# Attention, a dense feed-forward layer and routed experts in one kernel: weights joined in PSUM, the first tiles reordered, w_out split later, P of four tiles turned by TensorE

## The chip, the cores and the metric

One core of one Trainium2 chip runs the whole program. The metric is the device time of one execution in microseconds; the time before is 1401.77 us, the median of three runs (1400.38 to 1402.29).

## The reference, cut to what matters

```
# attention: B=8, H=8, S=576, D=64; k and v are averaged over runs of 8 rows (72 remain)
scores = matmul(q, mean8(k).T) / 8 ; attn = softmax(scores) ; x = attn @ mean8(v)     # x: 4608 x 512
# dense layer: w_in 512 x 2048, w_out 2048 x 512
h = x @ w_in ; g = where(h >= 1, h, where(h <= -1, 0, (h+1)**2 / 4)) ; x = g @ w_out
# routed layer: 8 experts, 512 -> 1024 -> 512, each token goes to the expert of its largest logit
out = gate * (relu(x @ w1[e]) @ w2[e])
```

The weights w_in and w_out arrive as 64-bit floats. The kernel reads them as two 32-bit words and makes a 32-bit float of each pair itself.

## The kernel before, in words

The 4608 tokens are 36 tiles of 128, in ten blocks (`BLK`): three tiles, seven blocks of four, three, two. A product in 32-bit accuracy is three matmuls: every operand is kept as a high and a low part, and high by high, high by low and low by high are added up.

**Blocks.** For block j and each of the 16 slices m of the hidden width, `f1(j, m)` is the first product (12 matmuls, L593 to L595) with its activation: L600 on VectorE, L601 on ScalarE, L605 on VectorE, L606 on ScalarE (high part) and `low_part`, L264, on VectorE. `f2(j, m)` is the second product (L621 to L623). The loop over `steps` calls `f1` two steps ahead of `f2`; between them `slot` puts in the attention of the next block's tiles (`units`), conversions of weights, and routing. Called functions append work to `later` and `pend`; `flush` and `mix` issue it. That writing order is the order in each engine's queue.

**A tile's attention** (`tile_units`): `u_qt` transposes q, `u_sc_all` makes the scores (L312), takes maxima and differences on VectorE (L319, L321) and the exponential on ScalarE (L326); `finish` sums (L376), adds 1e-9 (L378), takes the reciprocal (L379) and multiplies (L382 or L390 on GpSimd); P is transposed; `u_pv` multiplies by V (L425) and writes the block's input XT, high part on ScalarE (L431), low part on VectorE (L432). Two ways exist to transpose P. `u_pt` uses TensorE (L412) and ScalarE (L414). `u_turn_p` and `u_place_p` use two VectorE block transposes (L396, L398), a store to DRAM (p_d) and three loads back. `turned(t)` chooses: through DRAM for tiles 3 to 6 and 9 to 33.

**Weights** are converted in block 0 and ahead of it, 32 pieces in the table `order`: w_in 0 to 3, w_out 0 and 1, and so on. For piece n, `tick` issues `convert_a(n)` on ScalarE (L527: the high words, scaled, into the destination; L531: their signs), `convert_b(n)` on VectorE (L539: low word shifted and joined with the sign, both read from SBUF, written to the PSUM bank `CV`; L542: the destination shifted and joined with CV) and, for piece n-2, `convert_c` (L549 on ScalarE: high part; L264 on GpSimd: low part). For w_out both parts are also stored to DRAM (`wo_d`, 512 KB a piece), and from block 1 on `load_out` loads them for each slice.

**First tiles.** Tiles 0 to 2 come before any product of the dense layer. Keys and values are pooled by `head_pool` (L249 on VectorE, L252 to L254 on GpSimd) or by TensorE (`u_kp`), and five pieces of weights have been through `convert_a` when the first product starts.

Of the kernel before, what the change touches and what calls it, by code (L numbers as in the profile page):

```python
# [24 lines left out]
def attention_ffn_routed_experts_kernel(  # L25
# [12 lines left out]
    nc = tc.nc  # L38
# [70 lines left out]

    KB = [at(576 * i, 4 * SP_).rearrange("p (a c) -> p a c", a=4) for i in range(2)]  # L110
    QB = [at(1152 + 512 * i, 512) for i in range(2)]
    QB2 = at(6336, 512)
    QT = at(2176, 512)
    SC = [at(2688, 576), at(7616, 576)]
    HEAD = blocks[0][1]
    RAW = [at(3264 + 512 * i, 512, SP_) for i in range(3)]
    KP = at(4800, 512, SP_)
# [160 lines left out]
    def u_kp(b, c, raw):  # L278
# [25 lines left out]
    def u_sc_all(t):  # L304
        pbs = [bank(), bank()]
        for c in range(4):
            for g in range(2):
                toks = slice(64 * g, 64 * g + 64)
                kb = KB[(t * 128 + 64 * g) // S % 2]
                for i in range(2):  # L310
                    rows = slice(64 * i, 64 * i + 64)
                    nc.tensor.matmul(pbs[i][toks, c * SP_:(c + 1) * SP_],  # L312
                                     qt_of(t)[rows, c * 128 + 64 * g:c * 128 + 64 * g + 64],
                                     kb[rows, c], start=True, stop=True)
        sc, sc3, smx = sc_of(t), sc3_of(t), smx3[:, t % 3]
        for i in range(2):
            src = pbs[i][:, 0:4 * SP_].rearrange("p (h c) -> p h c", h=4)
            hs = slice(i, H, 2)
            nc.vector.tensor_reduce(out=smx[:, hs], in_=src, axis=AX.X, op=ALU.max)  # L319
            mix()  # L320
            nc.vector.tensor_tensor(out=sc3[:, hs], in0=src,  # L321
                                    in1=smx[:, hs].to_broadcast([128, 4, SP_]), op=ALU.subtract)
        wide[0] = True

        def exps():
            nc.scalar.activation(out=sc, in_=sc, func=ACTF.Exp, scale=1.0 / 64)  # L326
            finish(t)
# [195 lines left out]
    def convert_a(i):  # L523
        dst, rb = cvt_dst(i)
# [8 lines left out]
    def convert_b(i):  # L533
# [572 lines left out]
    with tc.manual_schedule():  # L1106

        wgp = WG.rearrange("p e d -> p (e d)")[0:SP_]
        raw0 = [WG[0:SP_, i] for i in range(8)] + RAW + [
            FX[0:SP_, 512 * i:512 * (i + 1)] for i in range(1, 5)] + [PT[:, 0]]  # L1110
# [5 lines left out]
        def run_units(n):  # L1116
            for _ in range(n):
                units.popleft()[1]()
            if qloads:
                qloads.popleft()()  # L1120

        load_q(0)
        for i in range(H):
            load_kv(0, i, raw0[i])
        load_q(1)
        load_q(2)
        for i in range(H, 2 * H):
            load_kv(0, i, raw0[i])
# [23 lines left out]
        hu[2][2]()
        head_pool(15, nc.gpsimd)
        for i in (11, 13):
            head_pool(i, nc.vector)
# [5 lines left out]
        line = [(0, 3), (0, 5), (1, 3), (0, 6), (1, 5), (2, 3), (1, 6), (2, 5), (2, 6)]
        for i, (t, n) in enumerate(line):
            hu[t][n]()
            flush()
            if i in (0, 2, 4, 6):
# [291 lines left out]
```

## Time and profile before

| | |
|---|---|
| median of three runs | 1401.77 us |
| the profiled execution's own time | 1404.79 us |
| span of its profile | 1402.8 us |
| TensorE matmul busy | 1357.5 us, 97% |
| VectorE, ScalarE, GpSimd busy | 778.1, 433.7, 358.7 us |
| first product starts | 38.11 us |
| block 1's first product starts | 146.73 us |

The page's second part cuts the span into 40 slices of 35 us. TensorE's busy tenths begin 6, 8, 7, 8 and are 9 from there to the last slice, which is 8. In a row of the timeline the columns are: start in us, duration in us, engine, line, operation, output and input, shape, count, and in brackets the idle time before and what ended it.

### The profile page before, as it was taken

How to read it: one execution, taken by the hardware profiler on the slowest of the kernel's cores; microseconds unless marked ns; L12 is line 12 of the kernel's file. 1: busy time of each engine (PE TensorE's matmuls, PEld its weight loads, DVE VectorE, ACT ScalarE, POOL GpSimd, SP SyncE). 2: the span in 40 equal slices, each digit the busy share in tenths (PEclk: the TensorE clock that was granted, in tenths of full speed). 3: DMA queues.
4: the chain of work that ended last, by engine and by line, in shares of the span. 5: the costliest groups of instructions: out<-in, count | busy, mean ns of one | idle time of the engine just before them, and what ended most of it. 6: DMA issues, size and time to landing. Idle time of an engine off the chain costs nothing. (4 is left out here: it accounts for less than half of the span.)

```text
span 1402.8 us, 22101 instructions
## 1 busy us (share of the span) xinstructions
PE 1357.5 (97%) x8082; PEld 1112.8 (79%) x8082; DVE 778.1 (55%) x1577; ACT 433.7 (31%) x729; POOL 358.7 (26%) x520
## 2 busy tenths in 40 slices
PE   6878999999999999999999999999999999999998
PEld 4767778878878778788788888888878888888786
DVE  5798556565666666575666556455532333323426
ACT  4567332222222222223222223343111111111335
POOL 5384736004304203413310011022221211111212
PEclk9999999999999999999999999999999999999999
DMA  9786647436636555545553344572543223331235
GB/s 254 226 261 240 182 136 214 129 122 194 164 124 187 153 149 168 171 155 143 165 157 111 98 152 130 192 263 72 195 129 106 91 74 113 99 111 61 79 127 187
DMA packets 170701, 213.45 MB, mean 152 GB/s; under 512 B 83432, under 2 KB 114440, under 8 KB 170569
## 3 DMA queue, kind: packets, MB, share of 16 engines
q1 hardware_dynamic: 135992, 102.29, 25.2%
q10 hardware_dynamic: 26784, 88.16, 18.8%
q0 software_dynamic: 7792, 21.35, 4.8%
q8 instruction: 69, 1.13, 0.3%
q14 instruction: 64, 0.52, 0.1%
HBM read 188.30 MB, written 47.03 MB: 168 GB/s over the span
## 5 line engine op out<-in xcount | busy, mean ns | idle before, releaser
L593 PE MATMUL ps<-XT,W 128*128 128x512 f32 (+2 forms) x640 | 243.8, 381 | 6.8 <-DVE FG L264 3.0
L595 PE MATMUL ps<-XT,W 128*128 128x512 f32 (+2 forms) x640 | 237.9, 372 | 2.7 <-POOL W L264 2.7
L594 PE MATMUL ps<-XT,W 128*128 128x512 f32 (+2 forms) x640 | 238.1, 372 | 0.2 <-DVE XT L432 0.2
L621 PE MATMUL ps<-WO,FG 128*128 128x512 f32 x576 | 231.6, 402 | 1.3 <-ACT FX L601 1.1
L622 PE MATMUL ps<-WO,FG 128*128 128x512 f32 x576 | 225.9, 392 | 0.0
L623 PE MATMUL ps<-WO,FG 128*128 128x512 f32 x576 | 225.2, 391 | 0.0
L601 ACT ACTIVATE FX<-FX,half 128x512 f32<-128x512 f32 (+2 forms) x152 | 104.0, 684 | 386.0 <-DVE FX L600 348.2
L600 DVE TENSOR_SCALAR FX<-ps 128x512 f32<-128x512 f32 (+2 forms) x152 | 96.7, 636 | 117.7 <-PE ps L595 116.9
L593 PEld LDWEIGHTS ps<-XT,W 128*128 128x128 f32 x640 | 121.8, 190 | 32.1 <-issue 3.4
L719 POOL DMA_INDIRECT perm_d<-idt,POSI x36 | 35.2, 978 | 417.6 <-DVE SM L705 353.0
L993 DVE SCALAR_TENSOR_TENSOR FG<-ps,FG 128x512 fp32r<-128x512 f32 (+1 forms) x64 | 43.2, 675 | 175.4 <-ACT FG L992 172.9
L595 PEld LDWEIGHTS ps<-XT,W 128*128 128x128 f32 x640 | 121.7, 190 | 22.3 <-POOL W L264 4.0
L605 DVE TENSOR_TENSOR ps<-FX,ps 128x512 f32<-128x512 f32 (+2 forms) x152 | 97.5, 641 | 72.8 <-ACT FX L601 71.4
L594 PEld LDWEIGHTS ps<-XT,W 128*128 128x128 f32 x640 | 121.7, 190 | 17.8 <-DVE XT L432 0.5
L621 PEld LDWEIGHTS ps<-WO,FG 128*128 128x128 f32 x576 | 108.5, 188 | 26.4 <-issue 3.0
L623 PEld LDWEIGHTS ps<-WO,FG 128*128 128x128 f32 x576 | 108.6, 188 | 23.7
L606 ACT ACTIVATE FG<-ps 128x512 fp32r<-128x512 f32 (+2 forms) x160 | 88.8, 555 | 123.9 <-DVE ps L605 112.2
L264 DVE TENSOR_TENSOR FG<-ps,FG 128x512 fp32r<-128x512 f32 (+2 forms) x160 | 100.8, 630 | 44.3 <-ACT FG L606 40.6
L622 PEld LDWEIGHTS ps<-WO,FG 128*128 128x128 f32 x576 | 108.7, 189 | 19.8
L252 POOL TENSOR_TENSOR AT<-AT 72x256 f32<-72x256 f32 x106 | 81.2, 766 | 136.3 <-DMA AT<-in_v_dram 68.7
L992 ACT ACTIVATE FG<-ps 128x512 fp32r<-128x512 f32 (+1 forms) x64 | 37.4, 584 | 244.8 <-PE ps L989 231.2
L987 PE MATMUL ps<-XT,W 128*128 128x512 f32 (+1 forms) x256 | 98.9, 386 | 2.9 <-ACT XT L971 2.5
(230 smaller groups left out, 2176.0 us busy)
## 6 DMA issues: line engine op xcount, KB each, us to landing
WO<-wo_d ACTq DMA_DIRECT2D x144, 512.0 KB
AT<-in_moe_w_dram SPq DMA_DIRECT2D x30, 1024.0 KB
p_d<-AT SPq DMA_DIRECT2D x29, 384.0 KB
AT<-in_v_dram SPq DMA_DIRECT2D x59, 144.0 KB
wo_d<-WO SPq DMA_DIRECT2D x16, 512.0 KB
AT<-in_k_dram SPq DMA_DIRECT2D x56, 144.0 KB
PT<-p_d SPq DMA_DIRECT2D x58, 128.0 KB
yrow_d<-Y ACTq DMA_DIRECT2D x7, 1032.0 KB
```

Source lines behind the costliest of these rows:

```text
L264: eng.tensor_tensor(out=lo, in0=x, in1=r32(hi), op=ALU.subtract)
L593: nc.tensor.matmul(o, wi(m, 0, c), xh, start=(c == 0), stop=False)
L594: nc.tensor.matmul(o, wi(m, 0, c), xl, start=False, stop=False)
L595: nc.tensor.matmul(o, wi(m, 1, c), xh, start=False, stop=(c == KD - 1))
L600: nc.vector.tensor_scalar(r, o, -1.0, 1.0, op0=ALU.max, op1=ALU.min)
L601: nc.scalar.activation(out=r, in_=r, func=ACTF.Square, scale=0.5, bias=half)
L605: nc.vector.tensor_tensor(out=o, in0=r, in1=o, op=ALU.max)
L606: nc.scalar.activation(out=gh, in_=o, func=ACTF.Copy)
L621: nc.tensor.matmul(o, gh, WO[:, g % 4, 0], start=(m == 0), stop=False)
L622: nc.tensor.matmul(o, gh, WO[:, g % 4, 1], start=False, stop=False)
L623: nc.tensor.matmul(o, gl, WO[:, g % 4, 0], start=False, stop=(m == KF - 1))
L987: nc.tensor.matmul(o, e1(0)[:, c, ms], xh, start=(c == 0), stop=False)
```

## The change

It has five parts.

1. **Join in PSUM.** `convert_a`'s first operation writes CV (PSUM) in place of the destination. VectorE's first join then reads CV and the sign, its second reads the low word and CV. No VectorE operation there reads two operands from SBUF. There is one CV, so piece n's first ScalarE operation has to come after piece n-1's second join; `convert_ab` sees to that order and is issued from `later`.
2. **First tiles.** q of tile 2 and the scores of tiles 0 to 2 come before the values are pooled; four heads of V are pooled by TensorE (`u_vp`) and one head of K goes from GpSimd to VectorE; two pieces of weights are through `convert_a` before the last tile's XT, and three follow after the first product. 1e-9 stands as a 73rd column of the scores, so the addition L378 is gone in all tiles.
3. **w_out.** Block 0 stores the joined 32-bit weights (`wf_d`, 256 KB a piece). In block 1 `split_out` loads a piece, splits it (ScalarE, GpSimd) and stores both parts to `wo_d`; from block 2 on they are loaded as before.
4. **P of tiles 3 to 6** goes by `u_pt`: eight TensorE transposes and two ScalarE copies a tile, in place of two VectorE transposes and four DMAs.
5. The exponential of tiles 0 to 8 is issued from `later`.

```diff
 def turned(t):
-        return TURN0 <= t < TURN1 or HEAD <= t < HEAD + blocks[1][1]
+        return TURN0 <= t < TURN1
...
+    def u_vp(more):
+
+        pb = bank()
...
+            for r in range(8):
+                nc.tensor.matmul(dst, ident[0:SP_, 0:SP_], x[:, :, r], start=(r == 0),
+                                 stop=(r == 7))
+        nc.scalar.activation(out=VS[:, 0, 0:(n + 1) * D], in_=pb[0:SP_, 0:(n + 1) * D],
+                             func=ACTF.Copy)
...
         def rest():
-            nc.vector.tensor_reduce(out=ssm, in_=sc3, axis=AX.X, op=ALU.add)
-            mix()
-            nc.vector.tensor_scalar(ssm, ssm, 1e-9, None, op0=ALU.add)
+            nc.vector.tensor_reduce(out=ssm, in_=sc4_of(t), axis=AX.X, op=ALU.add)
+            if t >= HEAD:
+                mix()
             nc.vector.reciprocal(out=ssm, in_=ssm)
...
-        nc.scalar.activation(out=dst.rearrange("p (a x) -> p a x", a=8), in_=high,
+        nc.scalar.activation(out=CV.rearrange("p (a x) -> p a x", a=8), in_=high,
                              func=ACTF.Copy, scale=2.0 ** -112)
...
-            out=ci, in0=rb[:, :, :, 0], scalar=29, in1=sg, op0=ALU.logical_shift_right,
+            out=ci, in0=ci, scalar=3, in1=sg, op0=ALU.logical_shift_left, op1=ALU.bitwise_or))
+        pend.append(lambda: nc.vector.scalar_tensor_tensor(
+            out=di, in0=rb[:, :, :, 0], scalar=29, in1=ci, op0=ALU.logical_shift_right,
             op1=ALU.bitwise_or))
-        pend.append(lambda: nc.vector.scalar_tensor_tensor(
-            out=di, in0=di, scalar=3, in1=ci, op0=ALU.logical_shift_left, op1=ALU.bitwise_or))
+
+    def convert_ab(i):
+        mix(len(pend))
+        convert_a(i)
+        convert_b(i)
...
         if o:
-            nc.sync.dma_start(out=r32(wo_d[m]), in_=r32(WO[:, m % 4]))
+            nc.sync.dma_start(out=wf_d[m], in_=dst)
...
-        for f, i in ((convert_c, n - 2), (convert_a, n), (convert_b, n)):
-            if 0 <= i < len(order) and order[i]:
-                f(i)
+        if 0 <= n - 2 < len(order) and n != 3:
+            convert_c(n - 2)
+        if n < len(order):
+            later.append(lambda: convert_ab(n))
...
+    def split_out(g):
+
+        if g < 2 * KF - 2:
+            nc.scalar.dma_start(out=WOF[(g + 2) % 4], in_=wf_d[(g + 2) % KF])
+        if g >= KF:
+            hi, lo = WO[:, g % 4, 0], WO[:, g % 4, 1]
+            nc.scalar.activation(out=hi, in_=WOF[g % 4], func=ACTF.Copy)
+            low_part(lo, WOF[g % 4], hi)
+            nc.sync.dma_start(out=r32(wo_d[g % KF]), in_=r32(WO[:, g % 4]))
...
-            if KF <= g + 1 < len(steps):
+            if KF <= g + 3 <= 2 * KF + 1:
+                split_out(g + 1)
+            elif 2 * KF < g + 2 <= len(steps):
                 load_out(g + 1)
...
         for m in range(AHEAD):
             f1(0, m)
             flush()
-            tick()
+            while ticks[0] < CAHEAD + 2 + m:
+                tick()
+                flush()
```

In the changed kernel the lines are: L546 and L550 for L527 and L531, L558 and L560 for L539 and L542, L573 for L549, L342 for L326, L433 for L414, L450 and L451 for L431 and L432, L635, L636, L640, L641 for L600, L601, L605, L606, L267 for L264.

ScalarE at the first tiles, before, from the exponential of tile 2 (L326) on; Y, AT and WG hold raw words, W is a converted weight:

```order
L326 ACTIVATE AT<-AT 128x576
L527 ACTIVATE FX<-Y 128x512
L531 ACTIVATE WG<-Y 128x512
L414 ACTIVATE FX<-ps_79 72x512
L527 ACTIVATE FX<-Y 128x512
L531 ACTIVATE WG<-Y 128x512
L414 ACTIVATE FX<-ps_72 72x512
L414 ACTIVATE PT<-ps_73 72x512
L549 ACTIVATE W<-FX 128x512
L527 ACTIVATE FX<-AT 128x512
L531 ACTIVATE WG<-AT 128x512
L431 ACTIVATE XT<-ps_74 128x4x128
```

The same place in the changed kernel:

```order
L342 ACTIVATE AT<-AT 128x8x72
L433 ACTIVATE VS<-ps_73 72x512
L433 ACTIVATE FX<-ps_74 72x512
L450 ACTIVATE XT<-ps_75 128x4x128
L546 ACTIVATE ps_78<-Y 128x512
L550 ACTIVATE WG<-Y 128x512
L433 ACTIVATE PT<-ps_76 72x512
L433 ACTIVATE PT<-ps_77 72x512
L450 ACTIVATE XT<-ps_79 128x4x128
L573 ACTIVATE W<-FX 128x512
L433 ACTIVATE FX<-ps_80 72x512
L433 ACTIVATE FX<-ps_73 72x512
```

Three pairs of conversions stood ahead of tile 0's XT copy (L431); none stands ahead of it now (L450), and one pair follows. ps_78 is CV.

ScalarE in block 0, before, from the high part of slice 7's activation (L606) to that of slice 8:

```order
L606 ACTIVATE FG<-ps_73 128x384
L326 ACTIVATE AT<-AT 128x576
L549 ACTIVATE W<-FX 128x512
L527 ACTIVATE FX<-Y 128x512
L531 ACTIVATE WG<-Y 128x512
L601 ACTIVATE FX<-FX,half 128x384
L549 ACTIVATE WO<-FX 128x512
L527 ACTIVATE FX<-AT 128x512
L531 ACTIVATE WG<-AT 128x512
L368 ACTIVATE AT<-ps_78 128x512
L606 ACTIVATE FG<-ps_72 128x384
```

The same step in the changed kernel:

```order
L641 ACTIVATE FG<-ps_74 128x384
L546 ACTIVATE ps_78<-Y 128x512
L550 ACTIVATE WG<-Y 128x512
L342 ACTIVATE AT<-AT 128x8x72
L573 ACTIVATE W<-FX 128x512
L546 ACTIVATE ps_78<-Y 128x512
L550 ACTIVATE WG<-Y 128x512
L636 ACTIVATE FX<-FX,half 128x384
L573 ACTIVATE WO<-FX 128x512
L433 ACTIVATE PT<-ps_79 72x512
L641 ACTIVATE FG<-ps_73 128x384
```

The two pairs moved behind the high part and behind the weight's copy, both write ps_78, and a copy of P (L433) came in.

VectorE in the same step, before and then changed:

```order
L605 TENSOR_TENSOR ps_73<-AT,ps_73 128x384
L542 SCALAR_TENSOR_TENSOR FX<-FX,ps_77 128x512
L264 TENSOR_TENSOR FG<-ps_73,FG 128x384
L376 TENSOR_REDUCE ssm_125<-AT 128x8
L378 TENSOR_SCALAR ssm_125<-ssm_125 128x8
L379 RECIPROCAL ssm_125<-ssm_125 128x8
L600 TENSOR_SCALAR FX<-ps_72 128x384
L539 SCALAR_TENSOR_TENSOR ps_77<-Y,WG 128x512
L542 SCALAR_TENSOR_TENSOR FX<-FX,ps_77 128x512
L605 TENSOR_TENSOR ps_72<-FX,ps_72 128x384
```

```order
L640 TENSOR_TENSOR ps_74<-AT,ps_74 128x384
L558 SCALAR_TENSOR_TENSOR ps_78<-ps_78,WG 128x512
L560 SCALAR_TENSOR_TENSOR FX<-Y,ps_78 128x512
L267 TENSOR_TENSOR FG<-ps_74,FG 128x384
L395 TENSOR_REDUCE ssm_126<-AT 128x8
L398 RECIPROCAL ssm_126<-ssm_126 128x8
L635 TENSOR_SCALAR FX<-ps_73 128x384
L558 SCALAR_TENSOR_TENSOR ps_78<-ps_78,WG 128x512
L560 SCALAR_TENSOR_TENSOR FX<-Y,ps_78 128x512
L640 TENSOR_TENSOR ps_73<-FX,ps_73 128x384
```

L378 is gone, and both joins of a piece now stand together, between L640 and L267 and between L635 and L640.

## Rows read from the trace of the kernel before

**Rows 1.** Busy time by stretch: us; busy (count) of PE, PEld, DVE, ACT, POOL; PEclk; DMA; GB/s.

```profile
0.00:38.00 38.00, 23.60 (x246) 18.02 (x246) 22.22 (x41) 18.57 (x35) 19.40 (x34) 1.00 0.87 241
38.10:150.00 111.90, 94.21 (x722) 78.22 (x723) 93.35 (x151) 72.72 (x133) 64.98 (x71) 0.94 0.74 237
180.00:200.00 20.00, 20.00 (x158) 15.79 (x158) 11.86 (x21) 6.16 (x11) 8.96 (x18) 1.00 0.51 145
```

**Rows 2.** Waits of PE, 38 to 150 us: total us, times, longest.

```profile
PE ps L425 <- DMA PT<-p_d: 6.2, 3, 3.5
```

**Rows 3.** Groups of VectorE instructions, 38 to 150 us: busy us, mean ns, idle before.

```profile
L542 DVE SCALAR_TENSOR_TENSOR FX<-FX,ps 128x512 int32<-128x512 int32 x28 | 19.2, 686 | 1.5
...
L378 DVE TENSOR_SCALAR ssm<-ssm 128x8 f32<-128x8 f32 x5 | 5.8, 1164 | 0.2
...
L396 DVE STREAM_TRANSPOSE AT<-AT 128x512 f32<-128x512 f32 x4 | 2.8, 704 | 0.0
L398 DVE STREAM_TRANSPOSE AT<-AT 128x256 f32<-128x256 f32 x4 | 1.6, 402 | 0.0
```

**Rows 4.** Busy time of L539 alone, 38 to 150 us: us, DVE busy (count).

```profile
38.00:150.00 112.00, 28.54 (x28) 0.94 0.74 238
```

**Rows 5.** Timeline of the first tiles, PE, VectorE and ScalarE.

```profile
12.78 0.38 PE L291 MATMUL ps<-ident,AT 72*128 72x72 f32 x1 [0.73 <-POOL AT L254]
...
17.81 1.02 DVE L249 TENSOR_REDUCE VS<-AT 72x64 f32<-72x512 f32 x1
...
20.68 0.67 DVE L378 TENSOR_SCALAR ssm<-ssm 128x8 f32<-128x8 f32 x1
...
23.30 0.69 ACT L326 ACTIVATE AT<-AT 128x576 f32<-128x576 f32 x1 [4.20 <-DVE AT L321]
...
36.74 0.60 ACT L431 ACTIVATE XT<-ps 128x512 fp32r<-128x512 f32 x1 [1.22 <-PE ps L425]
...
38.11 0.69 PE L593 MATMUL ps<-XT,W 128*128 128x384 f32 x1 [1.42 <-DVE XT L432]
```

**Rows 6.** Timeline of ScalarE, from the high part of slice 1 on.

```profile
47.47 0.49 ACT L606 ACTIVATE FG<-ps 128x384 fp32r<-128x384 f32 x1 [0.63 <-DVE ps L605]
47.85 0.62 ACT L549 ACTIVATE WO<-FX 128x512 fp32r<-128x512 f32 x1
48.37 0.68 ACT L527 ACTIVATE FX<-Y 128x512 f32<-128x512 f32 x1
48.95 0.79 ACT L531 ACTIVATE WG<-Y 128x512 f16<-128x512 f32 x1
49.59 0.60 ACT L601 ACTIVATE FX<-FX,half 128x384 f32<-128x384 f32 x1
```

**Rows 7.** Timeline of VectorE in block 0.

```profile
44.02 0.69 DVE L539 SCALAR_TENSOR_TENSOR ps<-WG 128x512 int32<-128x512 int32 x1
44.75 0.69 DVE L542 SCALAR_TENSOR_TENSOR FX<-FX,ps 128x512 int32<-128x512 int32 x1
45.35 0.55 DVE L600 TENSOR_SCALAR AT<-ps 128x384 f32<-128x384 f32 x1
...
63.14 0.54 DVE L605 TENSOR_TENSOR ps<-AT,ps 128x384 f32<-128x384 f32 x1
...
72.58 0.45 DVE L319 TENSOR_REDUCE smx<-ps 128x4 f32<-128x288 f32 x1
73.07 0.46 DVE L321 TENSOR_TENSOR AT<-ps,smx 128x288 f32<-128x288 f32 x1
73.44 0.45 DVE L319 TENSOR_REDUCE smx<-ps 128x4 f32<-128x288 f32 x1
...
128.70 0.55 DVE L605 TENSOR_TENSOR ps<-FX,ps 128x384 f32<-128x384 f32 x1
```

**Rows 8.** Timeline of PE at the end of block 0.

```profile
133.18 0.73 PE L312 MATMUL ps<-AT 64*64 64x72 f32 x32
...
146.73 0.50 PE L593 MATMUL ps<-XT,W 128*128 128x512 f32 x1 [0.48 <-ACT XT L431]
```

**Rows 9.** Groups of ScalarE instructions, 38 to 150 us.

```profile
L368 ACT ACTIVATE AT<-ps 128x512 f32<-128x512 f32 x6 | 3.4, 566 | 0.0
```

**Rows 10.** Groups of GpSimd instructions, 38 to 150 us.

```profile
L264 POOL TENSOR_TENSOR WO<-FX,WO 128x512 fp32r<-128x512 f32 x16 | 20.7, 1296 | 26.9 <-ACT WO L549 23.3 <-PE ps L622 3.6
```

More of the change, by code (lines that the diff above doesn't have):

```diff
@@ L73, in attention_ffn_routed_experts_kernel @@
     wo_d = dram.tile([KF, 128, 2, DM], F32R, name="wo_d")
+    wf_d = dram.tile([KF, 128, DM], F32, name="wf_d")
     yrow_d = dram.tile([NT + 128, ROW], F32, name="yrow_d")
@@ L108, in fx @@
         return FX[:, o:o + n]
-    KB = [at(576 * i, 4 * SP_).rearrange("p (a c) -> p a c", a=4) for i in range(2)]
-    QB = [at(1152 + 512 * i, 512) for i in range(2)]
+    KB = [at(288 * i, 4 * SP_).rearrange("p (a c) -> p a c", a=4) for i in range(2)]
+    QB = [at(1160 + 512 * i, 512) for i in range(2)]
     QB2 = at(6336, 512)
-    QT = at(2176, 512)
-    SC = [at(2688, 576), at(7616, 576)]
+    QT = at(7616, 512)
+    SCW = H * (SP_ + 1)
+    SC = [at(2184, SCW), at(576, SCW)]
     HEAD = blocks[0][1]
-    RAW = [at(3264 + 512 * i, 512, SP_) for i in range(3)]
+    RAW0 = 3264
+    RAW = [at(RAW0 + 512 * i, 512, SP_) for i in range(3)]
     KP = at(4800, 512, SP_)
@@ L286, in u_kp @@
         nc.scalar.activation(out=KB[b][:, c], in_=pb[:, 0:SP_], func=ACTF.Copy)
+    def u_vp(more):
+        pb = bank()
+        n = len(RAW)
+        raw = at(RAW0, n * 512, SP_).rearrange("p (h r d) -> p h r d", h=n, r=8)
+        for x, h0, h1 in ((raw, 0, n), (more.rearrange("p (h r d) -> p h r d", h=1, r=8), n, n + 1)):
+            dst = pb[0:SP_, h0 * D:h1 * D].rearrange("p (h d) -> p h d", h=h1 - h0)
+            for r in range(8):
[3 more added lines that the diff above has]
+                             func=ACTF.Copy)
     def u_kt_pair(b, c):
@@ L325, in exps @@
         def exps():
-            nc.scalar.activation(out=sc, in_=sc, func=ACTF.Exp, scale=1.0 / 64)
+            nc.scalar.activation(out=sc3, in_=sc3, func=ACTF.Exp, scale=1.0 / 64)
             finish(t)
-        if HEAD <= t < TURN0:
+        if t < TURN0:
             later.append(exps)
@@ L1108, in attention_ffn_routed_experts_kernel @@
         wgp = WG.rearrange("p e d -> p (e d)")[0:SP_]
-        raw0 = [WG[0:SP_, i] for i in range(8)] + RAW + [
+        raw0 = [WG[0:SP_, i] for i in range(6)] + [VS[:, 1], PT[:, 1]] + RAW + [
             FX[0:SP_, 512 * i:512 * (i + 1)] for i in range(1, 5)] + [PT[:, 0]]
@@ L1120, in run_units @@
                 qloads.popleft()()
+        nc.gpsimd.memset(WG[:, 6:8], 0.0)
+        for t in range(3):
+            nc.gpsimd.memset(sc4_of(t)[:, :, SP_:SP_ + 1], 1e-9)
         load_q(0)
@@ L1126, in attention_ffn_routed_experts_kernel @@
         load_q(2)
-        for i in range(H, 2 * H):
+        for i in (12, 13, 8, 9, 10, 11, 14, 15):
             load_kv(0, i, raw0[i])
@@ L1133, in attention_ffn_routed_experts_kernel @@
             u_kp(0, c, wgp[:, 1024 * c:1024 * (c + 1)])
-        for i in (4, 5):
+        for i in (4, 5, 6):
             head_pool(i, nc.vector)
-        for i in (6, 7):
-            head_pool(i, nc.gpsimd)
-        nc.gpsimd.memset(WG[:, 6:8], 0.0)
+        head_pool(7, nc.gpsimd)
         for i in range(3, NRB):
@@ L1143, in attention_ffn_routed_experts_kernel @@
             u_kt_pair(0, c)
-        for i in (8, 10, 12):
+        for i in (12, 13, 14):
             head_pool(i, nc.gpsimd)
         hu[0][2]()
+        hu[2][0]()
+        later.popleft()()
         hu[1][2]()
-        hu[2][0]()
-        head_pool(9, nc.vector)
-        head_pool(14, nc.gpsimd)
+        rest = later.popleft()
+        later.popleft()()
+        rest()
+        head_pool(15, nc.gpsimd)
+        later.popleft()()
+        hu[2][2]()
+        exps2 = later.popleft()
+        tick()
         flush()
[L1152 to L1155, printed above, removed]
+        u_vp(raw0[11])
+        exps2()
         load_pair(0)
         load_pair(1)
+        hu[0][3]()
+        flush()
+        hu[0][5]()
+        hu[0][6]()
+        tick()
+        flush()
+        hu[1][3]()
+        hu[1][5]()
+        hu[1][6]()
+        tick()
+        hu[2][3]()
+        hu[2][5]()
+        convert_c(1)
+        hu[2][6]()
         flush()
         tick()
+        flush()
         kv = deque([pair_step(c) for c in range(4)] + [kv_step(1, i) for i in range(H, 2 * H)])
[L1161 to L1165, printed above, removed]
-                tick()
-        while ticks[0] < CAHEAD + 1:
-            tick()
         banks.clear()
```

19 lines of the change are left out of this document (11 added, 8 removed).

## The prediction

> **What bounds the kernel now.** I read the busy time by stretch first [rows 1]. From 160 us on TensorE has no gap (20.00 of 20.00 in the stretch shown), so a change pays only by bringing forward the moment at which that begins. Ahead of it lie two stretches: the first tiles, to 38.11 us [rows 5], and block 0. In block 0 TensorE is busy 94.21 of 111.90 us and VectorE 93.35. TensorE's largest wait there, 6.2 us in three pieces, is for P's way through DRAM [rows 2]. VectorE's groups come next [rows 3, 4]: L542, with one operand in SBUF and one in PSUM, takes 0.69 us each time; L539 reads two operands from SBUF and takes 28.54 / 28 = 1.02; L378, a sum over 8 numbers, takes 1.16. So block 0 is held by VectorE, whose work is inflated by 28.54 - 28 x 0.69 = 9.2 us in L539 and some 5 us in L378, and beside it by the waits for P.
>
> The timelines then give prices [rows 6, 7]. On ScalarE starts follow each other by 0.38 us after L606, 0.52 after L549, 0.58 after L527, 0.64 after L531, which ends 0.79 after its start. On VectorE L542 starts 0.73 after the L539 it depends on and frees the engine 0.60 later. A dependent start comes 0.04 after the end it waits for (L319 to L321).
>
> **First tiles.** Before, tile 2's exponential starts at 23.30 [rows 5]. The second transposition of K waits 0.73 less at most, since GpSimd pools one head where it pooled two; VectorE has no V head (1.02) and no L378 (0.67 for one, three in all) between the scores: together about -2.6, so 20.7. From there to the end of the last XT copy ScalarE needed 37.34 - 23.30 = 14.0. Five conversion pairs (0.58 + 0.64 each) and three weight copies (0.52) lay in it; one pair and two copies are left: -5.4. New is the wait for CV: piece 1's pair may start only when VectorE has joined piece 0, and that join stands behind tile 0's XT low part; I count 2.4 us of ScalarE idle for it and for P's transpositions. So 20.7 + 11.0 = 31.7, and the first product starts near 32.3: **-5.8**. Bounds -3 (the DMAs of V or raw weights late, 0.87 busy there) and -7.
>
> **What becomes of the lead.** The pieces that were converted ahead now stand behind it, and through the one CV they form a chain: ScalarE pair 0.58 + 0.79, hand-over, two joins 0.73 + 0.69, hand-over: 2.87 us a piece, in which neither engine can work ahead. Before, ScalarE wrote into separate destinations and only its throughput counted (0.52 + 0.58 + 0.64 = 1.7). From 31.7 to the start of piece 7 there are five such rounds, and in two of them a product's L640 and L641 step between, 1.0 each: 31.7 + 14.4 + 2.0 = 48.1. Before, piece 7 started at 48.37 [rows 6]. Of 5.8 us a lead of **0.3** is left, between +1.5 and -1.5 as TensorE runs slice 3.
>
> **A step of block 0.** Two pieces are converted in each of the first twelve steps. The chain is pair, joins, pair, joins, then L640 and L641: 1.37 + 0.04 + 1.42 + 0.04 + 1.37 + 0.04 + 0.73 + 0.60 + 0.55 + 0.04 + 0.38 = 6.6 us. A tile takes three steps and adds to the chain its maxima and differences (0.49 + 0.37 twice = 1.7 [rows 7]), 0.6 for XT's low part, 0.3 of the sum that isn't covered, and something new: the next tile's scores need the PSUM bank in which P's first half waits for its ScalarE copy, which stands behind the pair and two other operations; scores end 0.73 us [rows 8] after that copy, 0.9 after VectorE is free. 19.7 + 3.5 = 23.3 a tile; in the first of the three tiles from slice 3 to slice 12 the copy comes early, 22.4. Sum 69.0. Before, the same nine steps took 128.70 - 63.14 = 65.56 [rows 7]: **+3.4**, though VectorE itself has less to do (no L378, no transposes of 0.70 and 0.40, no inflated L539).
>
> One price isn't in the trace: ScalarE writing 128x512 to PSUM. With one side in PSUM it took 0.57 as a reader [rows 9]; L527 takes 0.68 [rows 6]. I take the middle, -0.055 for 18 pairs: **-1.0**, bounds 0 and -2. (The Trainium skill, "ScalarE: Activation LUTs", Step-by-step, says ScalarE writes faster to PSUM than to SBUF. No row here shows such a write; it gives no figure.)
>
> **End of block 0 and later.** From slice 12's L605 to block 1's first product it was 146.73 - 128.70 = 18.0 [rows 7, 8]. By the same chain: a step with scores 8.3, one without 6.9, then 3.9 without conversions, as P's second copy, L636 and a weight copy stand ahead of the XT copy: 19.1, **+1.1**. P's 32 TensorE transposes and the DRAM waits of 6.2 us fall into TensorE's idle time, since it waits for the chain; their cover gone, the transposes would cost some 4 to 7 us.
>
> In block 1 the split adds 16 ScalarE copies, 16 GpSimd subtractions of 1.30 us [rows 10], a load of half the size and a store on SP's queue. Each is written three steps ahead of its use, and ScalarE and GpSimd are under half busy [rows 1]: nothing, and at worst a few us where GpSimd stands before a V load with a subtraction behind it. SP's loads of q, K and V stand behind the stores, which wait for GpSimd. L378's removal in later tiles lies beside TensorE: nothing.
>
> **Sum**: -0.3 + 3.4 - 1.0 + 1.1 = +3.2 against the profiled execution's 1404.79, so 1408.0; that one lies 3.0 above the median of 1401.77, so **1404.9**. Its own range, by the bounds of lead, PSUM write and bank wait, is 1401.5 to 1408.5.
>
> **Rivals.** *A: the chain is a little shorter*, with the bank wait hidden (two times 0.9) and a PSUM write of 0.57 (-1.0 more): 1404.9 - 2.8 = 1402.1, no change. For it speaks that both are small things a row could hide; against, that a walk over queues forgets waits rather than invents them. Chance 0.25.
>
> *B: VectorE's relief is passed on.* The mechanism: if a round of CV takes under 2.6 us where I have 2.87, a step falls to 6.1, block 0 keeps its old pace and the first tiles' 5.8 us stay: 1396.0; the point is that 2.6. For it: VectorE was the bound, 14 us of its work were pure waiting and 6.2 us of TensorE's waits go. Against: the pair and the joins can't overlap, by the order shown. (The Trainium skill, "SBUF — State Buffer", SBUF: two separate sides, says that a VectorE operation with two SBUF inputs and a GpSimd operation shut each other out for a whole instruction. The trace agrees: L539 1.02, L542 0.69. By that rule alone the time would fall by up to those 14 us, to 1388.) Chance 0.19.
>
> *C: block 1 is late.* If w_out's low part, behind a waiting load on GpSimd, comes after TensorE in four of 16 steps by 2 us, 8 more: 1413. It decides where a V load takes longer than two steps. Chance 0.06.
>
> **Chances.** The forecast has 0.50. A measurement of this kernel tells about 0.2%, 2.8 us, from no change. Faster by more than that: B and a sliver of A, 0.21; within it: the rest of A and the forecast's lower end, 0.32; slower: 0.47. The range reaches from B's time to the forecast's upper end and half of C: 1396 to 1411.
>
> **What would show it.** First product near 32 us; L558 and L560 0.69 us without exception; ScalarE's L546 waiting for L560 some 1.4 us, again and again, in block 0; piece 7 near 48 us; nine steps from slice 3 in about 68; TensorE's L425 no longer waiting for DRAM; block 1's first product near 150. Wrong if ScalarE is not found waiting for VectorE's second join, or if block 1's first product comes before 145.

## The result and the profile after

The changed kernel takes 1414.72 us (median of 4 runs, 1412.2 to 1416.04) against 1402.03 for the kernel before: ratio 1.0091, 95% interval 1.0073 to 1.0108. It is slower by 12.7 us, where 3.2 were forecast. The profiled execution took 1412.2 us with a span of 1410.5.

Busy time by stretch, up to the first product, from there to block 1's first product, and in the stretch that answers to the last of [rows 1]; columns as there:

```profile
0.00:32.30 32.30, 22.31 (x278) 18.39 (x278) 14.74 (x31) 14.52 (x28) 14.91 (x29) 0.95 0.91 250
32.30:154.00 121.70, 95.70 (x742) 80.92 (x742) 78.33 (x141) 81.83 (x148) 58.68 (x67) 0.89 0.58 174
180.00:200.00 20.00, 18.51 (x154) 14.45 (x153) 8.32 (x14) 6.93 (x13) 11.04 (x17) 1.00 0.66 166
```

Block 0 lasts 121.7 us where it lasted 108.6 (146.73 less 38.11), and VectorE is busy 78 us in it, where [rows 1] had 93 in 111.9. In the last stretch TensorE has a gap that it did not have. The groups of VectorE from 38 to 154 us, answering to [rows 3, 4], say what VectorE did instead:

```profile
L558 DVE SCALAR_TENSOR_TENSOR ps<-ps,WG 128x512 int32<-128x512 int32 x28 | 19.5, 697 | 27.4 <-ACT WG L550 27.4
L560 DVE SCALAR_TENSOR_TENSOR FX<-WG,ps 128x512 int32<-128x512 int32 x15 | 10.3, 688 | 1.0
...
L335 DVE TENSOR_REDUCE smx<-ps 128x4 f32<-128x288 f32 x10 | 4.5, 451 | 2.5 <-PE ps L328 2.5
L635 DVE TENSOR_SCALAR AT<-ps 128x384 f32<-128x384 f32 x8 | 4.3, 544 | 5.1 <-PE ps L630 5.1
```

The joins take 0.70 and 0.69 us, L539's inflated 1.02 is gone and L378 with it, as planned. But VectorE stands idle 27.4 us ahead of the first join, all of it for ScalarE's L550. The kernel before, 38 to 150 us, had 0.7 us of idle time ahead of its first joins:

```profile
L539 DVE SCALAR_TENSOR_TENSOR ps<-WG 128x512 int32<-128x512 int32 x14 | 14.8, 1056 | 0.3
L539 DVE SCALAR_TENSOR_TENSOR ps<-Y,WG 128x512 int32<-128x512 int32 x10 | 10.3, 1028 | 0.4 <-ACT WG L531 0.4
L539 DVE SCALAR_TENSOR_TENSOR ps<-AT,WG 128x512 int32<-128x512 int32 x4 | 3.5, 874 | 0.0
```

TensorE's waits from 60 to 165 us, where [rows 2] had 6.2 us for DRAM:

```profile
PE ps L328 <- ACT PT L433: 12.2, 3, 6.1
PE ps L628 <- DVE FG L267: 1.7, 1, 1.7
...
PE ps L444 <- ACT PT L433: 0.5, 1, 0.5
```

The forecast's landmarks on the three engines' timelines, answering to [rows 5, 6, 7, 8]:

```profile
32.32 0.44 PE L628 MATMUL ps<-XT,W 128*128 128x384 f32 x1 [0.70 <-ACT XT L450]
...
48.17 0.64 ACT L546 ACTIVATE ps<-Y 128x512 f32<-128x512 f32 x1 [0.32 <-DVE FX L560]
...
61.98 0.56 DVE L635 TENSOR_SCALAR AT<-ps 128x384 f32<-128x384 f32 x1 [5.10 <-PE ps L630]
64.76 0.54 DVE L640 TENSOR_TENSOR ps<-AT,ps 128x384 f32<-128x384 f32 x1
...
134.64 0.55 DVE L640 TENSOR_TENSOR ps<-FX,ps 128x384 f32<-128x384 f32 x1
...
154.00 0.49 PE L628 MATMUL ps<-XT,W 128*128 128x512 f32 x1
```

First product 32.32, piece 7 at 48.17, slice 3's L640 at 64.76, slice 12's at 134.64, block 1's first product at 154.00. Between the two profiled executions the change costs 7.4 us (1412.20 less 1404.79), and 7.3 of them are there at block 1's first product (154.00 less 146.73). How the nine steps between the two L640 pass shows in one piece of them, VectorE and ScalarE:

```profile
87.21 0.55 DVE L640 TENSOR_TENSOR ps<-FX,ps 128x384 f32<-128x384 f32 x1
89.53 0.70 DVE L558 SCALAR_TENSOR_TENSOR ps<-ps,WG 128x512 int32<-128x512 int32 x1 [1.77 <-ACT WG L550]
90.26 0.69 DVE L560 SCALAR_TENSOR_TENSOR FX<-WG,ps 128x512 int32<-128x512 int32 x1
...
87.79 0.49 ACT L641 ACTIVATE FG<-ps 128x384 fp32r<-128x384 f32 x1 [1.23 <-DVE ps L640]
88.18 0.62 ACT L546 ACTIVATE ps<-WG 128x512 f32<-128x512 f32 x1
88.73 0.76 ACT L550 ACTIVATE WG<-WG 128x512 f16<-128x512 f32 x1
...
90.98 0.63 ACT L546 ACTIVATE ps<-WG 128x512 f32<-128x512 f32 x1 [1.01 <-DVE FX L560]
```

Two waits take turns. VectorE is idle 1.77 us from L640 until ScalarE has done L641 and the pair L546, L550; then ScalarE is idle 1.01 until the second join. The first of these belongs to the order of issue: `convert_ab` is appended to `later` and so comes behind L641. The second belongs to the one CV.

Block 1, where the split of w_out is new:

```profile
186.09 0.71 DVE L377 STREAM_TRANSPOSE AT<-AT 128x512 f32<-128x512 f32 x1 [5.58 <-DMA AT<-in_q_dram]
190.27 0.70 DVE L686 STREAM_TRANSPOSE WG<-Y 128x512 f32<-128x512 f32 x1
...
191.03 0.87 PE L694 MATMUL ps<-WG 128*32 128x96 f32 x32 [1.49 <-DVE WG L686]
...
SPq L246 <- POOL AT L257: 18.5, 6, 5.5
SPq L620 <- POOL WO L267: 8.7, 4, 3.1
```

The last two rows are SyncE's queue, 140 to 200 us. The store of the split parts, L620, waits 8.7 us in it for GpSimd, and q's loads stand behind it. VectorE's transpose of q, L377, then waits 5.58 us for its load, with L686 behind it, and the logits' product L694 waits for L686.

### The profile page after: what moved, and what is told of

Its sections match the earlier page's. It is cut to its first block, busy times and chain, and to the rows that moved or that the text cites. A ratio compares the mean times of both kernels' runs of the same rounds, so it can differ in the third digit from the quotient of the medians.

```text
span 1410.5 us, 22210 instructions
## 1 busy us (share of the span) xinstructions
PE 1361.5 (97%) x8146; PEld 1119.3 (79%) x8146; DVE 756.0 (54%) x1531; ACT 447.1 (32%) x754; POOL 370.3 (26%) x533
## 3 DMA queue, kind: packets, MB, share of 16 engines
q1 hardware_dynamic: 136408, 103.74, 25.5%
## 5 line engine op out<-in xcount | busy, mean ns | idle before, releaser
L628 PE MATMUL ps<-XT,W 128*128 128x512 f32 (+2 forms) x640 | 243.2, 380 | 4.8 <-DVE FG L267 4.0
L630 PE MATMUL ps<-XT,W 128*128 128x512 f32 (+2 forms) x640 | 236.7, 370 | 0.0
L636 ACT ACTIVATE FX<-FX,half 128x512 f32<-128x512 f32 (+2 forms) x152 | 103.9, 683 | 373.3 <-DVE FX L635 348.3
L635 DVE TENSOR_SCALAR FX<-ps 128x512 f32<-128x512 f32 (+2 forms) x152 | 96.8, 637 | 117.6 <-PE ps L630 117.2
L628 PEld LDWEIGHTS ps<-XT,W 128*128 128x128 f32 x640 | 121.2, 189 | 29.0 <-ACT W L573 4.2
L640 DVE TENSOR_TENSOR ps<-FX,ps 128x512 f32<-128x512 f32 (+2 forms) x152 | 97.5, 642 | 72.9 <-ACT FX L636 72.9
L630 PEld LDWEIGHTS ps<-XT,W 128*128 128x128 f32 x640 | 121.2, 189 | 18.4 <-POOL W L267 0.2
L641 ACT ACTIVATE FG<-ps 128x512 fp32r<-128x512 f32 (+2 forms) x160 | 88.8, 555 | 130.3 <-DVE ps L640 122.2
L267 DVE TENSOR_TENSOR FG<-ps,FG 128x512 fp32r<-128x512 f32 (+2 forms) x160 | 100.8, 630 | 44.2 <-ACT FG L641 42.7
L255 POOL TENSOR_TENSOR AT<-AT 72x256 f32<-72x256 f32 x104 | 76.4, 734 | 104.3 <-DMA AT<-in_v_dram 57.8
```

What stands on the lines that cost most here:

```text
L267: eng.tensor_tensor(out=lo, in0=x, in1=r32(hi), op=ALU.subtract)
L628: nc.tensor.matmul(o, wi(m, 0, c), xh, start=(c == 0), stop=False)
L630: nc.tensor.matmul(o, wi(m, 1, c), xh, start=False, stop=(c == KD - 1))
L635: nc.vector.tensor_scalar(r, o, -1.0, 1.0, op0=ALU.max, op1=ALU.min)
L636: nc.scalar.activation(out=r, in_=r, func=ACTF.Square, scale=0.5, bias=half)
```

## The experiments

Five parts are separated: where ScalarE's pair is issued (late: behind L641; early: at the head of the half step), where the pieces are joined, how P of tiles 3 to 6 goes, where w_out is split, and the first tiles' order. The shorter sum (no L378) was not undone by itself; it goes with the first tiles' order here. Ratios are to the kernel before, measured beside each run (1401.7 to 1402.6 us). The table has the medians, and from one profiled execution of each the starts of the first product and of L640 (L605 in the kernel before) in slices 3 and 12, and the nine steps between them. Lines in the kernels that were edited can lie a few off; names here are those of the changed kernel.

| run | pair | join | P | split | time, us | first product | slice 3 | slice 12 | nine steps |
|---|---|---|---|---|---|---|---|---|---|
| before | early | SBUF | DRAM | block 0 | 1402.0 | 38.11 | 63.14 | 128.70 | 65.6 |
| changed | late | PSUM | PE | block 1 | 1414.7 | 32.32 | 64.76 | 134.64 | 69.9 |
| e1_p_dram | late | PSUM | DRAM | block 1 | 1419.3 | 32.59 | 65.87 | 135.77 | 69.9 |
| e3_old_join | late | SBUF | PE | block 1 | 1409.8 | 30.74 | 59.89 | 129.13 | 69.2 |
| e4_no_split | late | PSUM | PE | block 0 | 1412.2 | 35.02 | 68.53 | 138.43 | 69.9 |
| e5_head_only | late | SBUF | DRAM | block 0 | 1408.9 | 35.33 | 64.74 | 134.98 | 70.2 |
| e7_clock_fill | late | PSUM | PE | block 1 | 1415.0 | 34.18 | 66.57 | 136.06 | 69.5 |
| e8_scores_first | late | PSUM | PE, scores first | block 1 | 1416.7 | 34.60 | 68.14 | 138.29 | 70.2 |
| e9_old_join_scores_first | late | SBUF | PE, scores first | block 0 | 1404.8 | 33.70 | 64.89 | 134.65 | 69.8 |
| e11_pair_early | early | PSUM | PE | block 1 | 1415.3 | 33.82 | 66.69 | 138.67 | 72.0 |
| e12_join_head_pair_early | early | PSUM | DRAM | block 0 | 1406.2 | 32.61 | 65.33 | 131.79 | 66.5 |
| **e10_head_only_pair_early** | early | SBUF | DRAM | block 0 | **1397.6** | 31.12 | 60.40 | 125.56 | 65.2 |
| e14_p_pe_pair_early | early | SBUF | PE | block 0 | 1403.2 | 33.78 | 63.72 | 132.63 | 68.9 |
| e15_scores_first_pair_early | early | SBUF | PE, scores first | block 0 | 1400.5 | 30.75 | 58.97 | 126.75 | 67.8 |
| *first tiles as before:* | | | | | | | | | |
| e2_before_p_pe | early | SBUF | PE | block 0 | 1409.2 | 37.86 | 61.38 | 135.28 | 73.9 |
| e13_before_pair_late | late | SBUF | DRAM | block 0 | 1411.6 | 37.70 | 64.29 | 134.68 | 70.4 |

### First round: the joins, P, the clock

**P through DRAM again.**

```diff
-        return TURN0 <= t < TURN1
+        return TURN0 <= t < TURN1 or HEAD <= t < HEAD + blocks[1][1]
```

> The changed kernel with P of tiles 3 to 6 sent through DRAM again, all else as changed. Theory 1 (the joins through one CV hold ScalarE and VectorE together; TensorE then idles for ScalarE's late copies, and its granted clock falls): the waits of 6.1 and 4.7 us for L433 go, some wait for DRAM comes back, and the time falls by 2 to 6 us, to 1409 to 1413. Theory 2 (the chain through CV alone sets the pace, whatever TensorE waits for): within 2 us of 1414.7. Theory 3 (turning P on TensorE is what costs): nearly all of the loss goes, 1403 to 1406.

Measured 1419.3 us, 1.0127 of before (1.0110 to 1.0144), 4.6 more than the changed kernel. None of the three theories had it. The waits for L433 are gone from the trace and the nine steps still take 69.9, so in the changed kernel TensorE's bank wait was hidden. In the profiles the two lie 5.0 us apart. Of these, 1.6 are there at block 1's first product (155.59); behind it L694 waits 2.7 us in place of 1.5, and from 180 to 200 us the granted clock is 0.91 where it is 1.00 in the changed kernel's profile. What the rest is stays open.

**The kernel before with P on TensorE** (the same line, the other way).

> The kernel before with one edit: P of tiles 3 to 6 turned by TensorE. Theory 3: 4 to 10 us slower than before. Theories 1 and 2: without the chain ScalarE's copies come early enough and VectorE loses its transposes, so between 3 us faster and 1 slower.

1409.2 us, 1.0044 of before (1.0027 to 1.0061): 6.6 us slower on the same chip (before 1402.6). Theory 3 holds here. The row that was forecast at 0.9 us a tile, 60 to 150 us (L312, L414 are L328, L433):

```profile
PE ps L312 <- ACT PT L414: 12.1, 4, 5.4
```

**The old joins.**

```diff
-        nc.scalar.activation(out=CV.rearrange("p (a x) -> p a x", a=8), in_=high,
+        nc.scalar.activation(out=dst.rearrange("p (a x) -> p a x", a=8), in_=high,
...
-            out=ci, in0=ci, scalar=3, in1=sg, op0=ALU.logical_shift_left, op1=ALU.bitwise_or))
+            out=ci, in0=rb[:, :, :, 0], scalar=29, in1=sg, op0=ALU.logical_shift_right,
+            op1=ALU.bitwise_or))
...
-            out=di, in0=rb[:, :, :, 0], scalar=29, in1=ci, op0=ALU.logical_shift_right,
-            op1=ALU.bitwise_or))
+            out=di, in0=di, scalar=3, in1=ci, op0=ALU.logical_shift_left, op1=ALU.bitwise_or))
```

> The changed kernel with the old way of joining (ScalarE writes the pieces' high part to SBUF, VectorE joins raw low part and sign into CV, then both into the destination). Theories 1 and 2: ScalarE no longer waits for VectorE's second join, the lead of the first tiles is kept, 1395 to 1401. Theory 3: stays above 1408, with the waits for L433 as they are.

1409.8 us, 1.0055 (1.0035 to 1.0074): 4.9 better than the changed kernel, but 9 to 15 above what theories 1 and 2 gave. What theory 3 said came true: above 1408, with L328's waits for L433 as they were (12.0 us). Slice 3 comes 4.9 us earlier, and the nine steps take 69.2. So with the late pair the join in PSUM costs in and behind the first tiles, and hardly in the steps.

**Zeros for TensorE.**

```diff
+    FILLER = {3: 24, 5: 24, 6: 18, 7: 6}
...
     def u_sc_all(t):
+        for _ in range(FILLER.get(t, 0)):
+            nc.tensor.matmul(ps[2], ZERO, wi4(0, 0), start=False, stop=False)
```

> The changed kernel with extra TensorE products of zeros (added to an accumulator, so nothing changes in the result) in front of the scores of tiles 3, 5, 6 and 7: 24, 24, 18 and 6 of them, 0.23 us each at 2.4 GHz, where TensorE idles now. Theory 1: the granted clock stays near 1.00 behind them, where it was 0.50 at 53 to 62, 90 to 99 and 117 to 124 us; slice 3's L640 comes 2 us earlier, the nine steps take 1 us less, and the time falls by 3 to 6 us, to 1409 to 1412. Theory 2: the clock may rise, but the chain sets the pace, within 1.5 us of 1414.7; theory 3 the same.

1415.0 us, no change. The edit did what it was for: here are three stretches of the changed kernel, then of this one, by busy time (the granted clock is the third number from the end):

```profile
53.00:62.00 9.00, 7.61 (x76) 7.15 (x77) 3.55 (x8) 3.05 (x7) 1.27 (x1) 0.50 0.80 234
90.00:99.00 9.00, 5.18 (x40) 4.17 (x41) 5.44 (x11) 4.38 (x9) 5.44 (x8) 0.50 0.80 261
117.00:124.00 7.00, 6.45 (x45) 5.44 (x46) 3.85 (x8) 3.25 (x7) 1.30 (x2) 0.53 0.46 129
```

```profile
53.00:62.00 9.00, 6.89 (x84) 5.69 (x84) 5.21 (x10) 5.72 (x12) 2.57 (x2) 0.93 0.96 265
90.00:99.00 9.00, 8.15 (x64) 6.40 (x63) 5.91 (x11) 4.85 (x10) 7.07 (x12) 1.00 0.81 233
117.00:124.00 7.00, 5.03 (x44) 4.28 (x45) 3.63 (x8) 3.37 (x7) 1.27 (x1) 0.76 0.58 187
```

At 1.2 GHz (0.50) TensorE in these stretches only works slowly through time in which it would wait. The clock's part of theory 1 falls.

### Second round: split, bank, first tiles

**w_out split in block 0.**

```diff
-            nc.sync.dma_start(out=wf_d[m], in_=dst)
+            nc.sync.dma_start(out=r32(wo_d[m]), in_=r32(WO[:, m % 4]))
...
-            if KF <= g + 3 <= 2 * KF + 1:
-                split_out(g + 1)
-            elif 2 * KF < g + 2 <= len(steps):
+            if KF <= g + 1 < len(steps):
                 load_out(g + 1)
```

> The changed kernel with w_out split in block 0 and stored whole, as before. If the split is hidden, as the prediction had it: within 1 us of 1414.7. If its store holds up SyncE's queue, and with it q's loads, VectorE's transpose L377 and the turning of block 0's rows (L686): the wait of 1.5 to 2.7 us at L694 goes, and the time falls by 2 to 5 us, to 1410 to 1413.

1412.2 us, 1.0074 (1.0057 to 1.0091), 2.5 less than the changed kernel; L694 no longer waits. The two intervals overlap, so this pair alone doesn't show the cost. All profiles together do: from block 1's first product to the end the six executions with the split in block 1 take 1255.5 to 1259.9 us, mean 1258.0, the ten with it in block 0 take 1252.2 to 1257.6, mean 1255.2. The split isn't hidden.

**Scores ahead of P's first half** (the order of units in `weave` for tiles 3 to 6).

```diff
+            if HEAD <= t - 1 < HEAD + blocks[1][1]:
+                order = ((t, 1), (t, 2), (t - 1, 3), (t - 1, 4), (t - 1, 5), (t + 1, 0), (t - 1, 6))
```

> The changed kernel with the scores of tiles 4 to 7 ahead of the first half of P of the tile before, so that they don't wait for the bank which holds it. Bank wait: L328's 12.2 us for L433 go and the nine steps from slice 3 fall from 69.9 to 66 or 67, the time to 1411 to 1413. Chain through CV: L328 no longer waits, but the nine steps stay at 69 to 70 and the time within 1 us of 1414.7.

1416.7 us, 2.0 above the changed kernel and outside both cases, nine steps 70.2: L328's wait went, L431 got one of 13.2 us for VectorE in its place, and the pace stayed. With the old joins and the split in block 0 as well:

> The old way of joining, w_out split in block 0, and the scores ahead of P's first half; of the change only the first tiles' order, the sum without its extra step and P on TensorE are left. If bank wait, chain and split are the three costs, all three are gone: nine steps in 63 to 66, no wait at L694, 1396 to 1401. If P on TensorE costs by itself, whatever the order: nine steps at 69, 1404 to 1408.

1404.8 us, 1.0021 (1.0009 to 1.0032), nine steps 69.8: the second case, in steps and time. L431 now waits 12.8 us for VectorE. The pace of the steps is untouched, so with the late pair neither bank, join nor split sets it. P on TensorE was still left; the next run takes it out.

**Old joins, P through DRAM, split in block 0** (three of the edits above together).

> The old way of joining, w_out split in block 0, and P of tiles 3 to 6 through DRAM; of the change only the first tiles' order and the sum without its extra step are left. First product near 31, nine steps in 64 to 66, no wait at L694: if the first tiles' lead of 5 to 7 us is kept, 1395 to 1400; if VectorE takes it back in block 0, as before near 1402.

1408.9 us, 1.0047 (1.0030 to 1.0064). A miss, and the one that opened the case: of the change only the first tiles, the shorter sum and `convert_ab` in `later` are left, VectorE has less to do than before, and the nine steps take 70.2. What is left in them, by elimination, is the place of the pair.

### Third round: the place of the pair

This edit stands in e10, e11 and e12; e13 makes the opposite one in the kernel before.

```diff
-        if n < len(order):
+        if CAHEAD + 3 <= n < len(order):
+            convert_ab(n)
+        elif n < len(order):
             later.append(lambda: convert_ab(n))
```

> The kernel of the first tiles' order alone (old joins, P of tiles 3 to 6 through DRAM, w_out split in block 0) with the pair issued early from piece 8 on. Deferral: nine steps in 64 to 66 in place of 70.2, 1401 to 1405, and any gain of the first tiles' order shows now. CV or P on TensorE: as without the edit, 1408 to 1410.

1397.6 us (10 runs), 0.9964 of before (0.9952 to 0.9976): faster than both kernels by 4.1 and 17 us, better than was expected. Nine steps in 65.2.

> The kernel before with one edit the other way: from piece 8 on ScalarE's pair is deferred behind L605 and L606, as the change has it, with the old joins. Deferral: VectorE idles 1.8 us a step, nine steps in 68 to 71 in place of 65.6, 1405 to 1409. CV: no change, 1401 to 1403.

The mirror image: in the kernel before, the late pair alone costs 9.9 us: 1411.6, 1.0071 (1.0050 to 1.0092), 2.6 more than was expected, with the nine steps at 70.4. Its VectorE, then that of e10_head_only_pair_early, at the same slice (L613 there and L642 here are L640):

```profile
87.50 0.55 DVE L613 TENSOR_TENSOR ps<-FX,ps 128x384 f32<-128x384 f32 x1
89.84 0.70 DVE L539 SCALAR_TENSOR_TENSOR ps<-WG 128x512 int32<-128x512 int32 x1 [1.78 <-ACT WG L531]
```

```profile
83.11 0.55 DVE L642 TENSOR_TENSOR ps<-FX,ps 128x384 f32<-128x384 f32 x1
83.57 2.03 DVE L558 SCALAR_TENSOR_TENSOR ps<-WG 128x512 int32<-128x512 int32 x1
```

With the pair late the join takes 0.70 us and VectorE idles 1.78 for it. With the pair early there is no idle time, and though the join is inflated to 2.03, its end comes 2.5 us after L640's start in place of 3.0. Ahead of all first joins from 38 us to the end of block 0 VectorE idles 22.1 us in e13_before_pair_late and 4.1 in e10_head_only_pair_early.

> The changed kernel with w_out split in block 0, P of tiles 3 to 6 through DRAM, and the pair early from piece 8 on; of the change the join in PSUM, the first tiles' order and the shorter sum are left. Deferral: nine steps in 65 to 67, 1402 to 1407, 2 to 5 behind the same kernel with the old joins, since the first tiles still go through one CV. CV: nine steps at 69 to 70, 1409 to 1414.

1406.2 us, 1.0031 (1.0018 to 1.0043). One CV with the pair early: nine steps in 66.5. But against e10_head_only_pair_early, from which it differs in the join alone, it loses 8.6 us. Of the 6.5 between the two profiles 4.9 are there at slice 3, as between the changed kernel and e3_old_join, and 1.3 come in the nine steps.

> The changed kernel with one edit: from piece 8 on ScalarE's pair L546, L550 is issued at the head of the half step, as before, and not behind L640 and L641; the join stays in PSUM. If the deferred pair makes the steps serial (VectorE idle 1.8 us between L640 and L558 in each): that idle time goes, the nine steps take 66 to 67 in place of 69.9, 1409 to 1412. If the one CV does it, whatever the order: 69 to 70, 1413 to 1416.

1415.3 us, no gain. The time is the second theory's, but the nine steps, 72.0, are longer than either had. L328 now waits 15.8 us for L433 in four pieces, where it waited 12.2 in three. That this wait was hidden under the late pair is the likely reading; the scores ahead of P's first half, which would take it away, were not tried in this kernel.

### Fourth round: P on TensorE by itself

e10_head_only_pair_early with `turned` as the change has it, then with the scores first as well (both diffs stand above).

> As the kernel of the first tiles' order with the pair early (old joins, w_out split in block 0), but with P of tiles 3 to 6 turned by TensorE. If L328's wait for the bank that holds P's first half costs by itself: nine steps in 69 to 73 in place of 65.2, 1403 to 1407 in place of 1397.6. If turning P costs only together with the deferred pair: 64 to 66, within 2 us of 1397.6.

1403.2 us, 1.0005 (0.9995 to 1.0014), 5.6 more than with P through DRAM; nine steps 68.9, just under the first case; L328 waits 11.4 us.

> The same with the scores ahead of P's first half. If it is the bank, and the order frees it: nine steps in 63 to 66, 1394 to 1399. If ScalarE's late copies of P hold the tile however the bank is shared: nine steps in 68 to 72, 1402 to 1407.

1400.5 us, 0.9987 (0.9974 to 1.0000). The order gives 2.7 of the 5.6 back, barely clear of the noise, and lies between the two cases: L431 waits 9.1 us for VectorE's differences, nine steps 67.8. Not tried: a third bank, which block 0 doesn't have.

With the first tiles of the change all eight combinations have now run. The nine steps:

| pair | SBUF, DRAM | PSUM, DRAM | SBUF, PE | PSUM, PE |
|---|---|---|---|---|
| early | 65.2 | 66.5 | 68.9 | 72.0 |
| late | 70.2 | 69.9 | 69.2 | 69.9 |

A late pair sets the pace whatever stands beside it, so it is enough to explain the changed kernel's steps. It isn't the only thing that is enough: one CV and P on TensorE together make the steps as long without it, though each alone costs less.

## Why the prediction was wrong

The direction was right, the size was 3.2 for 12.7 us. In the mechanism, the step that failed is the chain that the one CV was said to form; in size, the lead, the price of P on TensorE, the split and the way from the profiled execution to the median. By its steps:

- **First tiles, -5.8: right in the profiled execution** (32.32 less 38.11; tile 2's exponential came at 20.66, forecast 20.7), too large as a mean. Seven profiled executions with these first tiles and the join in PSUM start the first product at 32.3 to 35.0, mean 33.6; the three with the old first tiles start it at 37.7 to 38.1, mean 37.9: -4.3. Up to 1.8 us of the spread are there at the first product with V (21.87 in the changed kernel, 23.63 in e4_no_split), with the clock at 1.00 in both: ScalarE's first pair, which stands ahead of V's copy, waits for its raw weights until 19.07 in one and 20.97 in the other. That is the late DMA of the prediction's bound. The other 0.9 are the clock's (last section).
- **"Of 5.8 us a lead of 0.3 is left": mis-sized by 1.9.** Piece 7 was put at 48.1 and came at 48.17. The walk stopped there. Two more pieces through CV and tile 3's scores follow before slice 3, which came at 64.76 and not 62.8. That it is the join: from first product to slice 3 it takes 32.4 us with it and 29.2 with the old one (e3, e10), 25.0 before.
- **"Through the one CV they form a chain": 69.0 for nine steps, nearly the right size (69.9) for the wrong reason.** The prediction summed pair, joins, pair, joins, L640, L641 in series and put it down to the one CV. The pair's place behind L641 is enough for the series: with separate destinations and the late pair the steps take 69 to 70 (e3, e5, e13), with one CV, P through DRAM and the early pair 66.5 (e12). That the sum came near is in part luck, and its signs (piece 7, L546 waiting for L560, the nine steps) couldn't tell the two causes apart. The **-1.0** for L546's faster write wasn't there: L546 lasts 0.62 to 0.65 us where L527 takes 0.65 to 0.69, but L550 starts 0.56 us after it, as L531 did after L527 (medians from 38 us to block 1's first product; the 0.58 of [rows 6] is one case). (The Trainium skill, "ScalarE: Activation LUTs", Step-by-step, has writes to PSUM faster; 0.63 for L546 against 0.68 for L527 [rows 6] agrees for the durations.)
- **End of block 0, 19.1: the right size** (154.00 less 134.64 is 19.4). The same end takes 16.0 us in e10 with the early pair.
- **P on TensorE, "0.9 us after VectorE is free": mis-sized.** By itself it costs 6.6 (e2) and 5.6 us (e14 less e10). In the change it lies under the late pair, where P through DRAM is even worse (e1); that is why the sum came near with a term so far off.
- **Split in block 1, "nothing": failed.** It costs some 2.5 to 3 us (e4, and the means of all profiles). What shows of it is the queue that the prediction named and left unpriced: SyncE, with q behind the stores, and L694's wait of 1.5 to 2.7 us. Rival C had the place, with another wait. The changed kernel's own profile shows little of it: behind block 1's first product it takes 0.4 us longer than the kernel before.
- **From the profiled execution to the median.** The forecast took over that the profiled execution lay 3.0 us above the median. The changed kernel's lies 2.5 below its own. That is 5.5 of the 9.8 us by which the forecast missed; lead and steps are 1.9 each. No row stood behind carrying the 3.0 over; the place of one execution among its like is chance.

Rival B set its condition on a round of CV. The old joins took that round away (e3) and the steps stayed at 69. (The Trainium skill, "SBUF — State Buffer", SBUF: two separate sides, has a VectorE operation with two SBUF inputs and a GpSimd operation shut each other out. The trace agrees: L558, with one input in PSUM, takes 0.69 to 0.70 us in all 28 places.) The 14 us of relief did not come out as time; VectorE's idle time ahead of L558 grew to 27.4 us.

The costs don't add up one by one, since late pair, bank wait and CV fill the same idle time. From 1397.6, one at a time: pair late +11.3 (e5), join in PSUM +8.6 (e12), P on TensorE +5.6 (e14); together with the split they make 17. They would add up to 25.5.

## What to carry to other kernels

When two in-order engines pass work back and forth, look first at where in the queue the producer's operation stands: a producer that is issued one half step ahead hides its latency, the same operation behind the step's own hand-over makes the step serial, and faster operations then only make idle time. Make sure of it by a run that moves nothing else, in the kernel before too. Undo a change in pairs: where two costs share one idle time, undoing either alone shows nothing, and a forecast with the wrong cause can still hit the size. A queue that gets a store in front of a load needs a price, even when every engine is half idle.

## What the runs showed of the hardware

The granted clock is worth nothing where TensorE waits anyway (e7_clock_fill). In the changed first tiles it counts. e3_old_join and e14_p_pe_pair_early have these first tiles and the old joins; TensorE in e3, then in e14, from its first product with V on (L630 there is L628):

```profile
22.55 0.66 PE L444 MATMUL ps<-VS 72*64 72x128 f32 x8 [1.44 <-ACT VS L433]
...
27.14 1.07 PE L431 MATMUL ps<-ident,AT 128*72 128x128 f32 x8
...
30.74 0.44 PE L628 MATMUL ps<-XT,W 128*128 128x384 f32 x1 [0.70 <-ACT XT L450]
```

```profile
22.99 1.12 PE L444 MATMUL ps<-VS 72*64 72x128 f32 x8 [0.18 <-ACT VS L433]
...
29.26 1.92 PE L431 MATMUL ps<-ident,AT 128*72 128x128 f32 x8
...
33.78 0.69 PE L630 MATMUL ps<-XT,W 128*128 128x384 f32 x1 [0.70 <-ACT XT L450]
```

In this stretch the granted clock is 1.00 in e3 and 0.50 in e14, and eight transposes take 1.07 and 1.92 us: 2.4 and 1.2 GHz. The stretch lasts 8.2 us in e3, and in e15 at 1.00 too; in e14 it lasts 10.8, and 10.7 and 10.8 in e5 and e9 at 0.50. So the low clock costs 2.6 us here. With the join in PSUM the clock fell within the stretch in all seven executions. It lasts 10.4 to 10.6 us where tile 1's product with V still ran at 2.4 GHz (the changed kernel, e1, e12) and 11.4 where that ran at 1.2 (e4, e7, e8, e11).

A granted clock of 1.00 in the profile's column is not always 2.4 GHz. TensorE in the kernel before:

```profile
28.62 1.92 PE L412 MATMUL ps<-ident,AT 128*72 128x128 f32 x8
...
40.84 0.53 PE L595 MATMUL ps<-XT,W 128*128 128x384 f32 x1
...
42.46 0.33 PE L595 MATMUL ps<-XT,W 128*128 128x384 f32 x1
```

[rows 1] gives 1.00 up to 38 us, but eight transposes take the 1.92 us of e14, and a matmul of the first product takes 0.53 us until 41.8 and 0.33 behind. So these first tiles ran at 1.2 GHz, as in e2 and e13, where the column says 0.50 and the first product comes at 37.86 and 37.70. No profile here has the old first tiles at 2.4 GHz, and whether their start hung on the clock is not shown; against it speaks that ScalarE has no idle time there from 23.30 to 35.52 us. What decides when the clock drops in one execution and not in the next, these runs don't tell.
